# Loading three quarters of a first input tile as rows, turning them on TensorE, and putting all first loads on one queue: a recommender cross network on one Trainium2 core

**Chip, cores, metric.** One core of one Trainium2 chip. The metric is the device time of the whole program in microseconds (us); lower is better. Before the change it was 2277.72 us, the median of three runs (2276.81 to 2277.87).

## The reference

Six layers of a deep-and-cross network on 16384 rows of 1024 features, all in bf16:

```python
B, Din, L = 16384, 1024, 6            # x0 [B, Din], ws [L, Din, Din], bs [L, Din]
x = x0
for l in range(L):
    proj = einsum('bd,de->be', x, ws[l]) + bs[l]
    x = x0 * proj + x
```

## The kernel before

A *unit* is one layer on 1024 rows (a pair of blocks of 512): 16 pairs by 6 layers, 96 units. The 1024x1024 product of a unit is done as seven half-size products P1 to P7 (a Strassen-like scheme), in which VectorE (DVE) forms sums T1 to T4 of input blocks and w5, w6, w7, w3 of weight blocks. This kernel keeps features on partitions, so the first input tile is loaded transposed, in four quarters.

```python
def ttop(name, o, a, b, o_, rd, wr, **kw):          # DVE sums; every tensor_tensor has one line in the profile
    add(name, lambda: tt(o, a, b, o_), rd, wr, **kw)

def group(name, w, bank, bname, rhs, rname, m, start, u=u):   # one product group: 4 matmuls of 128x512
    def fn():
        for k in range(KH):
            nc.tensor.matmul(bank[:], lhsT=wt[(u, w)][:, k, m * P:(m + 1) * P], rhs=rhs[:, k, :],
                             start=(start and k == 0), stop=(k == KH - 1), skip_group_check=True)
    add(name, fn, ...)
# ... cut ...
ttop("T1", T[1][:], B12, B11, SUB, [XI[0, 1], XI[0, 0]], ["T1"])
ttop("T2", T[2][:], B22, T[1][:], SUB, [XI[1, 1], "T1"], ["T2"])
ttop("T3", T[3][:], B22, B12, SUB, [XI[1, 1], XI[0, 1]], ["T3"])
# ... cut: P1, P2 and P5 need B11, B21 and T1; P6 needs T2; P7 needs T3 ...
for i in range(NDUMMY):                              # NDUMMY = 14: matmuls on zeros, one every 0.43 us until about 5.0 us, then every 0.22
    nc.tensor.matmul((pX + pA)[i % (2 * KH)][:], lhsT=zeros[:, 0:P], rhs=zeros[:], start=True, stop=True, ...)

def load_quarter(dh, n):
    nc.sync.dma_start_transpose(out=blk(x0Ts[0], dh, n), in_=x0[n * NB:(n + 1) * NB, dh * H:(dh + 1) * H])

nc.scalar.dma_start(b_rows[:], bs.rearrange("l (m p) -> (l m) p", p=P))
for w in ("1", "2"):
    nc.scalar.dma_start(wt[(0, w)][:], w_src(0, w))
load_quarter(0, 0)
load_quarter(1, 0)
load_quarter(0, 1)
for h in range(2):
    load_half("w12", h)
    load_half("4", h)
load_quarter(1, 1)
```

The order of instructions on each engine comes from a table of ranks, `name@time`. `P6.3` is the fourth group of P6; `2i5`, `2i7`, `2i6` are three small weight sums that later units need. The last unit turns half of its result back on TensorE and stores it in six transfers, of which three are issued last by the SP queue.

## Time and profile before

| | before |
|---|---|
| median time, us | 2277.72 |
| span of the profiled run | 2275.2 |
| PE (TensorE) busy | 2265.4 |
| first P6 matmul | 20.36 |
| issue of the last SP stores to the last byte | 5.36 |

The timeline of DVE (start, duration, engine, line, operation, shapes, and in brackets the idle time and what ended it):

```profile
12.66 1.23 DVE L198 TENSOR_TENSOR T<-x0T 128x2048 bf16<-128x2048 bf16 x1 [3.75 <-DMA x0T<-in_x_dram]
17.23 0.69 DVE L198 TENSOR_TENSOR wp<-w,wp 128x1024 bf16<-128x1024 bf16 x1 [1.70 <-DMA wp<-in_ws_dram]
19.09 1.22 DVE L198 TENSOR_TENSOR T<-x0T,T 128x2048 bf16<-128x2048 bf16 x1
```

These are T1, the second half of w5 and T2, which releases P6.

### The profile page before, as it was taken

Reading aid. Unit: us, or ns where it says so; the run is one execution under the profiler, and the core shown is the slowest. Engines: PE = TensorE matmul, PEld = TensorE weight load, DVE = VectorE, ACT = ScalarE, POOL = GpSimd, SP = SyncE. Lnnn points to the kernel's source line nnn. Section 1 sums busy time; section 2 is a strip of 40 time slices with the busy share of each in tenths; the row PEclk is TensorE's granted clock in tenths of the full one; section 3 lists DMA queues with packets and bytes.
Section 4 is the critical chain, followed back from the end, with each engine's and each line's share of the span. In section 5 each row is a group of like instructions: output and inputs, shape, how many; then the busy total and the mean of one; then the engine's idle time right before and its main releaser. Section 6 shows DMA issues by size and latency. Waiting matters only on the chain.

```text
span 2275.2 us, 34978 instructions
## 1 busy us (share of the span) xinstructions
PE 2265.4 (100%) x12951; PEld 1264.0 (56%) x12951; DVE 2079.9 (91%) x2326; ACT 1839.4 (81%) x3228; POOL 22.1 (1%) x43
## 2 busy tenths in 40 slices
PE   9999999999999999999999999999999999999998
PEld 4455555555555555555555555555555555555554
DVE  7999999999999999999999999999999999999997
ACT  5678888888888888888888888888888888888887
POOL 1110000000000000000000000000000000000000
PEclk9999999999999999999999999999999999999999
DMA  9779797796977969779697796978969689696872
GB/s 279 229 270 289 261 242 269 219 301 209 252 257 221 288 217 260 250 226 283 213 274 241 228 283 204 273 245 230 283 200 292 226 232 286 194 303 216 241 240 65
DMA packets 625868, 557.01 MB, mean 245 GB/s; under 512 B 397600, under 2 KB 552224, under 8 KB 625696
## 3 DMA queue, kind: packets, MB, share of 16 engines
q1 hardware_dynamic: 618864, 534.58, 79.1%
q0 software_dynamic: 5184, 18.88, 2.2%
q8 instruction: 101, 1.65, 0.3%
q10 hardware_dynamic: 1648, 1.32, 0.2%
q14 instruction: 71, 0.58, 0.1%
HBM read 436.22 MB, written 52.43 MB: 215 GB/s over the span
## 4 chain that ended last, share of the span: by engine, by line
PE 98%; DVE 1%; SPq 0%; DMA 0%; issue 0%; ACT 0%; DVEq 0%
PE pA L285 57%; PE pX L389 24%; PE pX L285 16%; DVE ev L198 1%; SPq L529 0%; DMA wp<-in_ws_dram 0%; DVE xst L198 0%; DVE T L198 0%; DVE ti L198 0%; DVE wp L198 0%; SPq L538 0%; ACT ev L294 0%; DVE x0T L487 0%; DVEq L608 0%; DVEq L198 0%
## 5 line engine op out<-in xcount | busy, mean ns | idle before, releaser
L285 PEld LDWEIGHTS <-wp 128*128 128x128 bf16 x7904 | 772.3, 98 | 843.7 <-issue 3.9
L285 PE MATMUL pA<-T,wp 128*128 128x512 bf16 x4608 | 1054.9, 379 | 0.5 <-DVE T L198 0.5
L294 ACT ACTIVATE ev<-pA,b_all 128x512 bf16<-128x512 f32 x1124 | 704.8, 690 | 211.8 <-PE pA L285 211.4
L389 PEld LDWEIGHTS <-wp 128*128 128x128 bf16 x4984 | 487.1, 98 | 156.6 <-issue 15.2
L198 DVE TENSOR_TENSOR ev<-ev,x0T 128x2048 bf16<-128x2048 bf16 (+2 forms) x484 | 482.7, 999 | 8.1 <-ACT ev L294 1.5
L198 DVE TENSOR_TENSOR xst<-ev,xst 128x2048 bf16<-128x2048 bf16 x319 | 388.9, 1219 | 18.6 <-DVE ev L198 0.5
L389 PE MATMUL pX<-ti,wp 128*128 128x256 bf16 x2848 | 397.6, 272 | 0.0
L198 DVE TENSOR_TENSOR ev<-ev,ev 128x2048 bf16<-128x2048 bf16 (+1 forms) x283 | 343.7, 1215 | 26.7 <-ACT ev L294 9.8
L294 ACT ACTIVATE ev<-pX,b_all 128x512 bf16<-128x512 f32 x412 | 289.4, 705 | 59.9 <-PE pX L285 49.3
L285 PE MATMUL pX<-xst,wp 128*128 128x512 bf16 x1376 | 336.4, 379 | 0.0
L285 PE MATMUL pA<-xst,wp 128*128 128x512 bf16 x1280 | 313.5, 379 | 0.0
L290 ACT COPY pX<-pA 128x512 f32<-128x512 f32 x412 | 256.3, 625 | 44.7 <-PE pA L285 44.3
L290 ACT CAST ev<-pX 128x512 bf16<-128x512 f32 x384 | 224.8, 619 | 49.0 <-ACT ev L294 37.6
L198 DVE TENSOR_TENSOR ev<-iu,ip 128x1024 bf16<-128x1024 bf16 x178 | 122.4, 688 | 120.7 <-ACT iu L290 120.7
L290 ACT COPY pX<-pX 128x512 f32<-128x512 f32 x356 | 208.7, 587 | 8.4
L290 ACT CAST iu<-pX 128x512 bf16<-128x512 f32 x356 | 196.8, 639 | 0.0
L198 DVE TENSOR_TENSOR T<-xst 128x2048 bf16<-128x2048 bf16 x160 | 194.8, 1217 | 0.3
L198 DVE TENSOR_TENSOR T<-xst,T 128x2048 bf16<-128x2048 bf16 x160 | 194.5, 1216 | 0.0
L389 PE MATMUL pX<-T,wp 128*128 128x256 bf16 x1068 | 160.2, 273 | 0.0
L290 ACT CAST ip<-pX 128x512 bf16<-128x512 f32 x178 | 104.7, 589 | 54.1 <-PE pX L389 54.1
L389 PE MATMUL pX<-xst,wp 128*128 128x256 bf16 x888 | 133.2, 273 | 0.0
L198 DVE TENSOR_TENSOR xst<-ev,x0T 128x2048 bf16<-128x2048 bf16 x64 | 78.2, 1222 | 1.6
(44 smaller groups left out, 624.3 us busy)
## 6 DMA issues: line engine op xcount, KB each, us to landing
wp<-Lc SPq DMA_DIRECT2D x538, 512.0 KB, 4.6
wp<-in_ws_dram SPq DMA_DIRECT2D x285, 512.0 KB, 5.3
out_dram<-x0T SPq DMA_DIRECT2D x30, 1024.0 KB, 8.6
Lc<-wp POOLq DMA_DIRECT2D x24, 512.0 KB, 6.2
Lc<-isum POOLq DMA_DIRECT2D x12, 512.0 KB, 6.9
w<-in_ws_dram SPq DMA_DIRECT2D x5, 512.0 KB, 6.3
wp<-in_ws_dram ACTq DMA_DIRECT2D x2, 512.0 KB, 5.8
out_dram<-x0T SPq DMA_DIRECT2D x2, 512.0 KB, 3.6
```

The costliest lines, as they stand in the source:

```text
L198: nc.vector.tensor_tensor(out=o, in0=a, in1=b, op=op)
L285: nc.tensor.matmul(bank[:], lhsT=wt[(u, w)][:, k, m * P:(m + 1) * P], rhs=rhs[:, k, :], start=(start and k == 0), stop=(k == KH - 1), skip ...
L290: add(name, lambda: nc.scalar.copy(out=dst, in_=src), rd, wr)
L294: add(name, lambda: nc.scalar.activation(out=dst, in_=src, func=IDENT, bias=b_all[:, c:c + 1], scale=1.0), rd, wr)
L389: nc.tensor.matmul(pX[bank][:, m * NQ:(m + 1) * NQ], lhsT=wv[:, k, m * P:(m + 1) * P], rhs=rhs[:, k, :], start=(start and m == 0 and k == ...
```

## The change

Intent: transposing loads are slow in this trace (245 against 357 GB/s, below), and they hold back the weights behind them. Three quarters of the tile are loaded as plain rows, and TensorE, which has holes at the start (3.2 us among the first 48 matmuls of products, below), turns them by multiplying with the identity. The weights w1 and w2 go between the row loads on the same queue, so that things arrive in the order in which they are used. Six of the 14 dummies go. In the table `t0.1` is a turn on TensorE and `u0.1` the copy of its result; `F` and `E` are ACT's operations on results of products.

```diff
-P1.1@-2.83 P1.0@-1.96 P1.2@-1.10 P1.3@-.24 P2.0@1.27 P2.1@3.53 ...
+t0.0@-4.00 u0.0@-3.70 t0.1@-3.80 u0.1@-3.50 ... t2.0@.3 t2.1@.4 t2.2@2.1 t2.3@2.2 u2.0@.5 ...
+P1.1@-2.83 bT@-2.4 P1.0@-1.96 P1.2@-1.10 P1.3@-.24 P2.1@1.27 P2.0@3.3 ...
-2i5@-9.73 T1@3.57 2i7@4.71 2i6@5.04 c5@5.67 c5b@7.37 c6@8.11 T2@9.25 c7@10.38 T3@11.52 ...
+T1@3.57 c5@5.67 c5b@5.8 c6@5.9 T2@9.25 2i5@9.3 2i7@9.4 2i6@9.5 c7@10.38 T3@11.52 ...
 ... cut: in the same table F1 and E2 are reordered ...
-    NDUMMY = 14
+    NDUMMY = 8
+    TURNED, rows = ((0, 0), (1, 0), (0, 1)), (P1s, U, V)
 ... cut ...
+            for i, (d, n) in enumerate(TURNED):
+                for k in range(KH):
+                    def turn(i=i, k=k, xb=xb):
+                        for j in range(KH):
+                            nc.tensor.matmul(pX[xb][:, j * P:(j + 1) * P], lhsT=rows[i][:, j, k * P:(k + 1) * P], rhs=ident[:], ...)
+                    add(f"t{i}.{k}", turn, [], [Xn[xb]])
+                    cp = nc.vector.tensor_copy if k % 2 else nc.scalar.copy
+                    add(f"u{i}.{k}", lambda ...: cp(out=blk(x0T, d, n)[:, k], in_=pX[xb][:]), ...)
 ... cut: the turn of the bias becomes an operation of the table ...
-    for w in ("1", "2"):
-        nc.scalar.dma_start(wt[(0, w)][:], w_src(0, w))
-    load_quarter(0, 0)
-    load_quarter(1, 0)
-    load_quarter(0, 1)
+    load_rows(0)
+    nc.sync.dma_start(wt[(0, "1")][:], w_src(0, "1"))
+    load_rows(1)
+    load_rows(2)
+    nc.sync.dma_start(wt[(0, "2")][:], w_src(0, "2"))
     for h in range(2):
         load_half("w12", h)
         load_half("4", h)
     load_quarter(1, 1)
```

More of the change, by code (lines that the diff above doesn't have):

```diff
@@ L48 @@
 EARLY = [ranks("""
-P1.1@-2.83 P1.0@-1.96 P1.2@-1.10 P1.3@-.24 P2.0@1.27 P2.1@3.53 P2.2@4.49 P2.3@5.35 P5.1@6.94 P5.0@7.81 P5.3@8.67
+t0.0@-4.00 u0.0@-3.70 t0.1@-3.80 u0.1@-3.50 t0.2@-3.60 u0.2@-3.30 t0.3@-3.40 u0.3@-3.10
+t1.0@-1.90 u1.0@-1.60 t1.1@-1.70 u1.1@-1.40 t1.2@-1.50 u1.2@-1.20 t1.3@-1.30 u1.3@-1.00
+t2.0@.3 t2.1@.4 t2.2@2.1 t2.3@2.2 u2.0@.5 u2.1@.6 u2.2@2.2 u2.3@2.3
+P1.1@-2.83 bT@-2.4 P1.0@-1.96 P1.2@-1.10 P1.3@-.24 P2.1@1.27 P2.0@3.3 P2.2@4.49 P2.3@5.35 P5.1@6.94 P5.0@7.81 P5.3@8.67
 P5.2@9.53 P6.3@10.52 P6.2@11.38 P6.0@12.24 P7.3@13.11 P6.1@13.97 P7.0@14.83 P4.3@15.70 P7.2@16.56 P7.1@17.42
 P4.0@18.29 P4.2@19.15 P4.1@20.01 P3.0@20.88 P3.1@21.74 P3.3@22.60 P3.2@23.47
-F1.0@-.89 E2.0@2.34 F1.1@2.91 F1.3@3.39 F1.2@3.87 E2.1@4.60 E2.2@5.56 E2.3@6.42 E5.3@9.74 E5.0@10.22 F.3@11.59
+F1.1@-.9 F1.0@-.8 F1.2@2.25 F1.3@2.35 E2.1@2.7 E2.0@4.60 E2.2@5.56 E2.3@6.42 E5.3@9.74 E5.0@10.22 F.3@11.59
 E5.2@12.07 E5.1@12.54 F.0@13.31 E7.3@14.18 F.2@14.75 F.1@15.23 E7.0@15.90 E4.3@16.77 E7.2@17.63 E7.1@18.49 E4.2@20.22
 E4.0@20.79 E4.1@21.36 E3.0@21.95 E3.1@22.81 E3.3@23.67 E3.2@24.54
-2i5@-9.73 T1@3.57 2i7@4.71 2i6@5.04 c5@5.67 c5b@7.37 c6@8.11 T2@9.25 c7@10.38 T3@11.52 T4@12.65 2i3@13.79 c3@14.12
+T1@3.57 c5@5.67 c5b@5.8 c6@5.9 T2@9.25 2i5@9.3 2i7@9.4 2i6@9.5 c7@10.38 T3@11.52 T4@12.65 2i3@13.79 c3@14.12
 Qm@15.26 5i5@17.53 Va@19.74 Qa@20.88 Vm@22.01 Wma@23.15 Wmb@23.75 Wx@24.49 Ua@25.63 Um@26.90 Ux@28.17 5i7@29.30
@@ L344, with turn_bias @@
         B11, B12, B21, B22 = blk(xs, 0, 0), blk(xs, 0, 1), blk(xs, 1, 0), blk(xs, 1, 1)
+        A = [f"A{m}" for m in range(KH)]
+        Xn = [f"X{m}" for m in range(KH)]
+        if first:
+            for i, (d, n) in enumerate(TURNED):
+                for k in range(KH):
+                    xb = k if i < 2 else 2 + k % 2
+                    def turn(i=i, k=k, xb=xb):
+                        for j in range(KH):
+                            nc.tensor.matmul(pX[xb][:, j * P:(j + 1) * P], lhsT=rows[i][:, j, k * P:(k + 1) * P], rhs=ident[:],
+                                             start=(j == 0), stop=True, skip_group_check=True)
+                    add(f"t{i}.{k}", turn, [], [Xn[xb]])
+                    cp = nc.vector.tensor_copy if k % 2 else nc.scalar.copy
+                    add(f"u{i}.{k}", lambda cp=cp, d=d, n=n, k=k, xb=xb, x0T=x0T: cp(out=blk(x0T, d, n)[:, k], in_=pX[xb][:]), [Xn[xb]], [Xn[xb], X0[d, n]])
+            def turn_bias():
+                nc.tensor.matmul(pA[KH - 1][:, 0:LK], lhsT=b_rows[:], rhs=ident[0:LK, 0:LK], start=True, stop=True, skip_group_check=True)
+                nc.vector.tensor_copy(out=b_all[:], in_=pA[KH - 1][:, 0:LK])
+            add("bT", turn_bias, [], [A[KH - 1]])
         ttop("T1", T[1][:], B12, B11, SUB, [XI[0, 1], XI[0, 0]], ["T1"])
@@ L348 @@
         ttop("T4", T[4][:], B21, T[2][:], SUB, [XI[1, 0], "T2"], ["T4"])
-        A = [f"A{m}" for m in range(KH)]
-        Xn = [f"X{m}" for m in range(KH)]
         if not one:
@@ L541, with load_rows @@
     nc.scalar.dma_start(b_rows[:], bs.rearrange("l (m p) -> (l m) p", p=P))
-    for w in ("1", "2"):
-        nc.scalar.dma_start(wt[(0, w)][:], w_src(0, w))
-    load_quarter(0, 0)
-    load_quarter(1, 0)
-    load_quarter(0, 1)
+    def load_rows(i):
+        d, n = TURNED[i]
+        nc.sync.dma_start(rows[i][:], x0[n * NB:(n + 1) * NB, d * H:(d + 1) * H].rearrange("(j p) d -> p j d", p=P))
+    load_rows(0)
[3 more added lines that the diff above has]
+    nc.sync.dma_start(wt[(0, "2")][:], w_src(0, "2"))
     for h in range(2):
@@ L550 @@
     load_quarter(1, 1)
-    nc.tensor.matmul(pA[KH - 1][:, 0:LK], lhsT=b_rows[:], rhs=ident[0:LK, 0:LK], start=True, stop=True, skip_group_check=True)
-    nc.vector.tensor_copy(out=b_all[:], in_=pA[KH - 1][:, 0:LK])
     writer, readers, succ, need = {}, {}, [[] for _ in ops], [0] * len(ops)
```

## The prediction

> **What bounds the kernel now.** I read the page first: TensorE (PE) is busy for the whole span, and the chain that ended last is almost all PE.
>
> ```profile
> span 2275.2 us, 34978 instructions
> ...
> PE 2265.4 (100%) x12951; PEld 1264.0 (56%) x12951; DVE 2079.9 (91%) x2326; ACT 1839.4 (81%) x3228; POOL 22.1 (1%) x43
> ...
> PE 98%; DVE 1%; SPq 0%; DMA 0%; issue 0%; ACT 0%; DVEq 0%
> ```
>
> The reader is to see that nothing outside the few microseconds where PE is not on the chain can be won: 2275.2 - 2265.4 = 9.8 us. Next, the view of who waited for whom, restricted to PE over the whole run, says where those are.
>
> ```profile
> PE pX L285 <- ACT pX L290: 1.3, 1, 1.3
> PE pX L526 <- DVE zeros L523: 1.2, 1, 1.2
> PE pA L285 <- DVE T L198: 0.5, 1, 0.5
> PE pX L285 <- DVE wp L198: 0.5, 1, 0.5
> PE pA L285 <- DMA x0T<-in_x_dram: 0.4, 1, 0.4
> ```
>
> Those are all of PE's waits, 3.9 us, and the timeline of PE puts every one before 20.4 us:
>
> ```profile
> 6.78 3.61 PE L285 MATMUL pA<-x0T,wp 128*128 128x512 bf16 x16 [0.36 <-DMA x0T<-in_x_dram]
> 10.52 1.02 PE L285 MATMUL pX<-x0T,wp 128*128 128x512 bf16 x4
> 12.81 2.85 PE L285 MATMUL pX<-x0T,wp 128*128 128x512 bf16 x12 [1.26 <-ACT pX L290]
> 15.59 1.90 PE L285 MATMUL pX<-T,wp 128*128 128x512 bf16 x8
> 17.98 1.90 PE L285 MATMUL pX<-T,wp 128*128 128x512 bf16 x8 [0.49 <-DVE wp L198]
> ```
>
> The columns are start, duration, and in brackets the idle time and what ended it. These are the products P1 (16 matmuls), P2 (16) and P5 (16) of the first unit; P6, the first that needs T2, starts at 20.36 us. Full-speed matmuls start every 0.216 us (the 48 of P6, P7 and P4 start at 20.36 and the next group at 30.72: 10.36 / 48), so these 48 need 10.4 us, yet take 13.58 us from 6.78. The 3.2 us between are what the change can aim at, and what runs before 6.78 (dummies on zeros, 1.19 to 6.2). The chain of waits for the first 31 us names the cause: the SP queue's transposing loads, then a weight load, then VectorE (DVE).
>
> ```profile
> 8.04 2.24 SPq L529
> ...
> 12.05 5.08 DMA wp<-in_ws_dram
> ...
> 17.23 0.70 DVE wp L198
> 17.95 1.23 DVE wp L198
> 19.18 1.15 DVE T L198
> ...
> 20.36 10.52 PE pA L285 x48
> ```
>
> DVE waited 3.7 us for the third transposed quarter (T1 starts at 12.66), then for the halves of w12 and 4, issued only behind the transposes at 10.33 to 12.05 (the first half of the sum w5 starts at 14.84, the second at 17.23); T2 ran at 19.09 and released P6.
>
> [...] In the windows view, 8 to 12 us holds almost only transposing loads and 22 to 30 only plain ones; the last columns are DMA share and GB/s:
>
> ```profile
> 8.00:12.00 4.00, 3.41 (x16) 1.30 (x14) 0.43 (x1) 0.99 (x2) 0.00 (x0) 1.00 1.16 245
> 22.00:30.00 8.00, 8.00 (x39) 3.60 (x37) 8.00 (x10) 6.02 (x11) 0.00 (x0) 1.00 1.09 357
> ```
>
> 245 against 357 GB/s: 512 KB takes 2.1 us transposing and 1.5 us as rows. [...] Here the dummies go every 0.43 us from 1.19 until about 5.0, then every 0.22: 3.8 us. [...] The last unit's transposes by identity agree: four start at 2267.46, the next four at 2267.68, 0.22 / 4 = 55 ns.
>
> **The change part by part.**
>
> *Loads.* Three transposing loads (3 x 2.1 us of DMA) become three row loads (3 x 1.5), and the SP order becomes rows 0, w1, rows 1, rows 2, w2, four half weights, last the one transposed quarter. SP issues take about 0.55 us each (0.51 to 0.58 in the timeline) against 1.5 us to move 512 KB, so DMA is the limit. A copy issued at 10.33 moved its first packets about 1.4 us later; so rows 0, issued at 0.74, should land near 4.1 and the others every 1.55 us: w1 5.6, rows 1 7.2, rows 2 8.7, w2 10.3, halves at 11.1, 11.9, 12.7, 13.5 (before: the last two needed by w5 let it start at 17.23). The transposed quarter adds 2.1 us and a gap of about 1 us: 16.5 (before: just ahead of T2 at 19.09).
>
> *Added on PE.* 3 x 16 = 48 transposes x 55 ns = 2.6 us, against six dummies fewer (14 to 8). The bias turn (0.2) only moves.
>
> *Added on ACT and DVE.* Twelve evictions of 128x512, six each. In the last unit such a cast takes 2.04 / 4 = 0.51 us on ACT and 1.88 / 3 = 0.63 on DVE: 3.1 and 3.8 us, in a stretch (0 to 20.36) where they were busy 7.13 and 6.59 us. ACT now interleaves them with the F1 copies.
>
> *The path in PE's order.* (1) Eight dummies, 1.19 + 8 x 0.427 = 4.6. (2) t0: 4 at half rate (0.43), 12 at 55 ns: 5.7. Its evictions alternate ACT and DVE and end near 6.7, so P1.1 finishes at 7.0 (start of the last matmul 6.8); before, its end was 6.78 + 0.86 = 7.64: only 0.6 us won so far. (3) Bias, P1.0: 8.0. (4) t1, 16 x 55 ns: 8.9. (5) P1.2, P1.3: 10.6. (6) Half of t2: 11.0, P2.1: 11.9 (w2 at 10.3 is in time). (7) Other half of t2, P2.0: 13.2. (8) P2.2 waits for F1.2, which stands on ACT behind the last evictions (12.3 + 0.5 + 0.6): 13.5, ends 14.4. (9) P2.3 15.2, then P5, four groups of 0.864: 18.7.
>
> *DVE beside it.* T1 needs all of t2, whose last eviction ends near 13.2. Full tensor_tensor operations start every 1.14 us: T1 13.2, two halves of w5 at 14.35 and 15.0, w6 15.75, T2 16.9 to 18.1. P5.1 (15.2) and P5.3 (16.9) find their weights ready, and P6 at 18.7 finds T2. T3, behind three small sums (3 x 0.335) and w7, ends near 21.4; P7.3, three groups after P6, wants it at 21.3: a wait of 0.1 us.
>
> *Sum.* P6 moves from 20.36 to about 18.7, less 0.1 us: 1.5 us won. After this PE never waited, so the shift should reach the end if DVE keeps up. DVE gains 1.4 us itself (T1 is later than 12.66 but the waits behind it vanish). The next unit's T1 ended at 40.31 and P5 began at 41.08, a slack of 0.77, more than the 0.1 to 0.3 by which PE may outrun DVE. Nothing in steady state or the tail changes. 2277.7 - 1.5 = 2276.2 us.
>
> **Rivals.**
>
> *A: the transposes take back what the loads give.* 2.6 us of added PE work is close to the 3.2 us of holes. For: they now stand between products, in PE's own order, and rows 0 need a load, a turn and an eviction before the first product. Against: the windows view has PE busy 3.61 of 5 us from 10 and 4.39 of 5.36 from 15, so 2.4 us are free there, and the six dropped dummies give room early. If evictions cost 0.3 us more per stage than I count: 2277.3 to 2277.9.
>
> *B: DVE becomes the bound.* It is busy 24.04 of 24.14 us in the stretch 20.36 to 44.5, so a PE that comes early may meet a DVE that doesn't: T1 starts 0.5 us later than before. For: DVE has no idle time there to catch up. Against: it was idle for 1.70 us before the second half of w5, which goes. PE would wait at P7.3 or the next unit's P5; gain limited to 0.8 us: 2276.9.
>
> *C: everything works as drawn, or better.* If P1.1 starts as soon as its evictions do and nothing waits, PE needs only 4.6 + 2.8 (turns) + 10.4 = 17.8: 2.5 us won, 2275.2. Against: the eviction wait after t0 (about 0.4 us) is in the dependencies.
>
> *D: a cold clock.* With six dummies fewer, the array may not have warmed when P1 starts; a matmul at half rate costs 0.21 us more[...]. For: activity has a hole between t0 and P1.1. Against: dummies and turns run without a break from 1.19 to 5.7, longer than the 3.8 us seen. [...]
>
> **Range and chances.** A and B shorten the gain to 0 to 0.8 us, C lengthens it to 2.5, and three runs before spread over 1.06 us (2276.81 to 2277.87). I take 2274.8 to 2277.7. Two per cent is 45 us, while all of PE's idle time is 9.8 us: faster or slower by over 2% is not credible, 0.5% each for a slow state or an accident.
>
> **What would show each step right or wrong.** Right: P6 (the first pA<-T matmul) starts at 18.2 to 19.2 rather than 20.36; no DVE wait for DMA after T1; PE has no wait after P7.3; the span is shorter by the same amount as P6 moved. Rows load near 350 GB/s. Wrong in the loads: PE waits for rows or w2 by DMA. Wrong in the turns: they start more than 60 ns apart, or PE waits for ACT or DVE evictions for over 1 us in all. Wrong in DVE: a wait for T3 or for T1 of the next unit, with P6 early but the end not. A prediction above 2277.7 would fall if the first P1 matmul came later than 6.8 us or ran at half rate.

2277.7 - 1.5 = 2276.2 us stands on times and rates of the trace before. Of these, the 55 ns of a turn come from the last unit alone, and the gap of about 1 us ahead of the transposed quarter is the stretch from 16 to 17 us, in which the windows view has 56 GB/s. That two weight loads moved to the SP queue change the order of arrival and not the rate was assumed, not shown. The range 2274.8 to 2277.7 was formed from A, B, C and the spread of the runs. That the clock hangs on unbroken work was D's assumption: the trace before shows the dummies every 0.43 us until about 5.0 us and every 0.22 after that.

## More of the kernel before

The timeline of the SP queue has the last stores, and the DMA view of 2262 to 2277 us has the packets moved there:

```profile
2268.22 1.96 SPq L491 DMA_DIRECT2D out_dram<-x0T  x3
```

```profile
DMA packets 5248, 2.62 MB, mean 175 GB/s; under 512 B 2176, under 2 KB 5248, under 8 KB 5248
```

These are all on two queues: 4720 on q1 (what SP issues) and 528 on q10 (what ACT issues).

## The result, and the profile after

The changed kernel took 2277.49 us, the median of four fast runs (2277.26 to 2277.73); the kernel before took 2277.26 in the same rounds (2276.79 to 2277.87). Ratio 1.0001, 95% interval 0.9984 to 1.0018: the same. A ratio here is the mean time of one kernel's fast runs over that of the other's fast runs of the same rounds, so it is not quite the ratio of the medians. The time lies inside the predicted range, but the gain of 1.5 us did not come.

First what holds. The page's head:

```profile
span 2275.9 us, 34833 instructions
...
PE 2254.5 (99%) x12754; PEld 1266.1 (56%) x12993; DVE 2084.2 (92%) x2332; ACT 1844.8 (81%) x3234; POOL 22.1 (1%) x43
```

PE's busy time and count are lower than before only because more matmul records are missing: the weight loads, one for each matmul, are 12993 against 12951, the 42 more that the diff adds (48 turns less 6 dummies). The waits of PE over the run, without the 1.2 us for the zeros at the start:

```profile
PE pX L359 <- DMA ev<-in_x_dram: 0.4, 1, 0.4
PE pA L289 <- DMA wp<-in_ws_dram: 0.4, 1, 0.4
PE pX L289 <- ACT pX L294: 0.2, 1, 0.2
```

With the zeros, four waits of 2.2 us against five of 3.9 us before. The timeline of PE (L359 are the turns, L289 the products):

```profile
5.18 1.07 PE L359 MATMUL pX<-ident,ev 128*128 128x128 bf16 x16 [0.40 <-DMA ev<-in_x_dram]
6.62 1.04 PE L289 MATMUL pA<-x0T,wp 128*128 128x512 bf16 x4 [0.38 <-DMA wp<-in_ws_dram]
...
14.18 1.89 PE L289 MATMUL pX<-x0T,wp 128*128 128x512 bf16 x8 [0.19 <-ACT pX L294]
15.91 3.62 PE L289 MATMUL pX<-T,wp 128*128 128x512 bf16 x15
19.36 4.89 PE L289 MATMUL pA<-T,wp 128*128 128x512 bf16 x21
```

P6, the first product with pA<-T, starts at 19.36 rather than 20.36: 1.0 us won. The chain of waits now begins with a weight load rather than a transposing one:

```profile
1.26 5.32 DMA wp<-in_ws_dram
```

It is w1, landed whole at 6.58. The windows view of the two stretches that the prediction compared:

```profile
8.00:12.00 4.00, 3.95 (x37) 2.56 (x37) 1.46 (x4) 2.41 (x5) 0.00 (x0) 1.00 1.14 322
22.00:30.00 8.00, 7.93 (x37) 3.63 (x38) 8.00 (x11) 5.78 (x11) 0.00 (x0) 1.00 1.09 351
```

(columns: stretch, its length, busy time of PE, PEld, DVE, ACT and POOL with counts, granted clock, DMA share, GB/s). 8 to 12 us moved 322 GB/s rather than 245. Next, a wait that the PE view hides: the timeline of PE's weight loads (PEld) shows the first group of P7 waiting for T3.

```profile
22.13 1.84 PEld L289 LDWEIGHTS <-wp 128*128 128x128 bf16 x10 [0.51 <-DVE T L202]
```

From there the lead is 0.81 us: the group that starts at 169.80 us in the kernel before starts at 168.99.

Now the end. The same views of the tail as before (timeline of SP, then the DMA view of 2262 to 2277 us):

```profile
2268.09 3.10 SPq L513 DMA_DIRECT2D out_dram<-x0T  x3
```

```profile
DMA packets 5249, 2.64 MB, mean 176 GB/s; under 512 B 2176, under 2 KB 5248, under 8 KB 5248
...
q8 instruction: 1, 0.02, 0.4%
```

The last stores are issued 0.13 us earlier than before, yet the packet records put the last byte at 2274.60 against 2273.58: 6.51 us after the issue rather than 5.36. (The issue of the three stores also takes 3.10 us rather than 1.96. In the eight traces with a long tail, listed below, it takes 1.97 to 3.10, in the others 1.93 to 1.96; why is not shown.) One thing is new: a single packet of 16 KB on q8, the queue that fetches instructions. The packet records show it at 2269.29, taking 0.95 us. TensorE has fetched its instructions in such packets all along, one for about 256 of them (25902 matmuls and weight loads, twice the count of loads, to 101 packets before, 25986 to 102 after): 101 before, the last at 2251.0; 102 after, with the last one among the final stores. (That this queue serves TensorE is borne out below: instructions added on TensorE change the count, to 102 in p1 and q1, those added on ACT and DVE do not, 101 in q4.) The windows view shows what is late, first before, then after:

```profile
2273.70:2276.00 2.30, 0.00 (x0) 0.00 (x0) 0.00 (x0) 0.00 (x0) 0.00 (x0) 0.50 0.00 0
```

```profile
2273.70:2276.00 2.30, 0.00 (x0) 0.00 (x0) 0.00 (x0) 0.00 (x0) 0.00 (x0) 0.68 0.03 8
```

After 2273.70 a share of 0.03 of 16 engines for 2.3 us is 1.1 us of one engine. One engine alone finishes about 1 us later than the others, the length of the fetch. (The records do not name the engine of a packet, so that it is the same one is an inference. It is the same in every trace: in the last 0.3 us before the last byte 14 packets end in each of the eight with a fetch there, 108 to 140 in each of the others.)

Between 180 us and the end the lead shrinks further. Comparing each ACT operation's time in the two traces gives eight small steps at fixed places: six of about +0.1 us (at 206, 578, 951, 1156, 1714 and 2066 us), and -0.26 at 1757 and -0.07 at 1985, in sum +0.33. (The rest of the shrinking, 0.36 us, is a slow drift: 23.451 us for a unit against 23.447. The record does not say on which chips these two traces were taken; between c1 and c2 below, on one chip, there is no drift.)

### The profile page after: what moved, and what is told of

Read it like the earlier page. It is cut to its first block, busy times and chain, and to the rows that moved or that the text cites. A ratio compares the mean times of both kernels' runs of the same rounds, so it can differ in the third digit from the quotient of the medians.

```text
span 2275.9 us, 34833 instructions
## 1 busy us (share of the span) xinstructions
PE 2254.5 (99%) x12754; PEld 1266.1 (56%) x12993; DVE 2084.2 (92%) x2332; ACT 1844.8 (81%) x3234; POOL 22.1 (1%) x43
## 3 DMA queue, kind: packets, MB, share of 16 engines
q8 instruction: 102, 1.67, 0.3%
## 4 chain that ended last, share of the span: by engine, by line
PE 98%; issue 1%; DVE 0%; DMA 0%; ACT 0%; DVEq 0%; SPq 0%; ACTq 0%
PE pA L289 57%; PE pX L411 24%; PE pX L289 17%; DVE ev L202 0%; DMA wp<-in_ws_dram 0%; ACT pX L294 0%; PE pX L359 0%; DVE xst L202 0%; DVE x0T L509 0%; ACT ev L298 0%; DVEq L633 0%; ACT x0T L363 0%; SPq L567 0%; PE pA L366 0%; ACTq L294 0%
## 5 line engine op out<-in xcount | busy, mean ns | idle before, releaser
L289 PEld LDWEIGHTS <-wp 128*128 128x128 bf16 x7904 | 772.3, 98 | 840.0 <-issue 1.2
L289 PE MATMUL pA<-T,wp 128*128 128x512 bf16 x4468 | 1047.2, 379 | 7.3
L202 DVE TENSOR_TENSOR xst<-ev,xst 128x2048 bf16<-128x2048 bf16 x319 | 389.1, 1220 | 19.1 <-DVE ev L202 0.9
L289 PE MATMUL pX<-xst,wp 128*128 128x512 bf16 x1371 | 335.9, 379 | 0.3
L289 PE MATMUL pA<-xst,wp 128*128 128x512 bf16 x1205 | 302.4, 379 | 3.9
```

Of the source, the lines that this page charges most:

```text
L202: nc.vector.tensor_tensor(out=o, in0=a, in1=b, op=op)
```

## The experiments

Each run has a short label (c1, p1 and so on), which the text uses from here on.

**Theory F.** The 102nd instruction fetch of TensorE falls among the last stores and costs about 1.0 us, so most of what the start wins is lost. **Rival R.** The longer tail comes from something else in the change (buffers, the order of work at the end). **Theory S**, on the eight steps: they come from the shifted number of ACT and DVE instructions, whose fetches fall elsewhere. P6 below always means the start of its first matmul, and the *tail* the time from the issue of the last SP stores to the last byte. The chips and rounds differ, so each run is compared with the runs of the kernel before that stand beside it.

Two controls ran first, with no edit: the kernel before (c1) and the changed kernel (c2).

> The kernel before, unchanged, as a control. Every theory: ratio 1.000 within 0.0003 of the kernel before; P6 starts near 20.4 us; no instruction fetch for TensorE after 2262 us; the last store's bytes move until about 2273.6 us. What it measures is the run to run noise (0.5 us or so) and how far unit periods (23.447 us here) drift from run to run with no change at all.

> The changed kernel, unchanged, on the same chip. Theory T (the start wins about 0.8 us, and an extra 16 KB instruction fetch for TensorE among the last stores takes about 1 us back[...]): first P6 near 19.4 to 19.5 us, fetch near 2269 us again, tail from the last TensorE matmul to the last byte 1 us longer than in the control, time within 0.3 us of the control. Rival R (the start's lead is lost by chance, slow drift of the unit period and a chance landing at the end): the lead at 180 us is again 0.8 us, no fetch at the end or a fetch without delay, and the time is 0.5 to 0.9 us below the control.

Measured: 2277.03 us for the kernel before (2276.90 to 2277.99), 2277.03 for the changed one (2276.88 to 2277.75), beside 2277.17 (2276.83 to 2277.72, nine runs) of the kernel before; ratio 1.0 for both, 0.9988 to 1.0013. By the traces, on one chip: P6 at 20.32 and 19.60; lead at 150 us 0.52, at the last weight load 0.27 (2269.10 against 2268.83), with the same eight steps between (in sum +0.30); SP issue to last byte 5.34 and 6.37. The tail difference of 1.03 us repeats; the last byte is 0.75 us later. The changed kernel starts better and ends worse. (c2's trace is of the slowest of its five runs, 2277.75 us, so this one is no typical run.)

**More TensorE instructions, nothing else (p1).** The kernel before with its 14 dummies cut into 56 shorter ones of the same total length:

```diff
-    for i in range(NDUMMY):
-        nc.tensor.matmul((pX + pA)[i % (2 * KH)][:], lhsT=zeros[:, 0:P], rhs=zeros[:], ...)
+    for i in range(56):
+        nc.tensor.matmul((pX + pA)[(i // 4) % (2 * KH)][:, 0:128], lhsT=zeros[:, 0:P], rhs=zeros[:, 0:128], ...)
```

> The kernel before with its 14 dummies of 512 columns cut into 56 of 128: the same TensorE time at the start, but 84 more TensorE instructions, exactly as many as the changed kernel has. Theory T: start as in the control (P6 near 20.4 us), but a 16 KB instruction fetch near 2269 us and the last store's bytes 0.7 to 1.0 us later; time 0.5 to 1.0 us above the control. Rival R: no longer than the control (within 0.3 us), since nothing but the dummies differs.

Measured: 2279.39 us (2279.32 to 2279.91) beside 2277.17; ratio 1.001 (0.9997 to 1.0024). The 102nd fetch is there at 2270.9, and the tail is 6.22 us. None of the eight steps appears, though the fetches have moved: for TensorE itself they cost nothing that shows after the start. A second effect is larger: the *first* fetch of TensorE moved from 28.0 to 19.1 us, into the load of the transposed quarter (1,1). T2 then waited 1.45 us for that load, of which 15 of 16 parts had landed by 19.58 and the last at 21.13, and the timeline of PE has

```profile
22.43 2.75 PE L285 MATMUL pA<-T,wp 128*128 128x512 bf16 x11 [2.04 <-DVE T L198]
```

P6 came 2.1 us later than in the control, which the expectation did not foresee. With the tail's 0.9 this is more than the 2.2 us of the medians. To the end of the span rather than to the last byte the tail costs only 0.44 us here (7.47 us from the issue against 7.03 in c1), and that with 2.1 makes the 2.57 us between the two spans. So 84 more instructions (42 matmuls and 42 weight loads), which compute nothing new, slow this kernel by 0.1%: the interval includes 1, but all five runs lie above all nine of the kernel before.

**The changed kernel with the fetch moved away from the tail (p2)**, by more instructions at the start:

```diff
-    for i in range(NDUMMY):
-        nc.tensor.matmul((pX + pA)[i % (2 * KH)][:], lhsT=zeros[:, 0:P], rhs=zeros[:], ...)
+    for i in range(72):
+        nc.tensor.matmul((pX + pA)[(i // 8) % (2 * KH)][:, 0:64], lhsT=zeros[:, 0:P], rhs=zeros[:, 0:64], ...)
```

> The changed kernel with its 8 dummies of 512 columns cut into 72 of 64 (until about 5 us instead of 4.6, where TensorE waited for rows anyway): 128 more TensorE instructions, so that the last instruction fetch comes 64 TensorE pairs earlier, near 2255 to 2263 us, ahead of the last stores. Theory T: first P6 within 0.2 us of the changed kernel, tail as short as in the control, time 0.6 to 1.1 us below the changed kernel and 0.5 to 1.0 below the control. Rival R: the same time as the changed kernel.

Measured: 2276.89 us (2276.74 to 2277.16) beside 2277.17. The last fetch is at 2256.7 and the tail 5.33 us: short again, with all else of the change in place. This speaks for F and against R. But rows 1 came late (PE waited 0.68 us for them until 9.17), P6 stood at 20.06, and the lead was only 0.06 us. The first fetch had come forward to 8.85 us, among the row loads, but it is not shown to be the cause: in b4 below the last of the 16 parts of rows 1 is as late (9.04 us, 0.87 after the one before it; here 9.12 and 0.86), and the first fetch there is at 16.6.

**The kernel before with instructions added only at the end (q1)**, after all work:

```diff
+    for i in range(42):
+        nc.tensor.matmul(pX[0][:, 0:32], lhsT=zeros[:, 0:P], rhs=zeros[:, 0:32], start=True, stop=True, ...)
```

> The kernel before with 42 tiny matmuls (84 TensorE instructions) appended after its last transposes, where TensorE has nothing to do while the last stores run. Theory T (extra fetch): nothing changes up to the last transpose (2269.1 us), but a 16 KB instruction fetch appears among the last stores and the time from the last transpose's weight load to the last store byte grows from 4.44 us to 5.2 to 5.7; time 0.7 to 1.2 us above the kernel before. Rival R (the longer tail of the changed kernel has to do with something else in it, such as the order of its stores' issues): tail 4.4 us and time within 0.3 us of before.

Measured: 2278.69 us (2277.94 to 2278.97) beside 2276.87 (2276.32 to 2277.69, nine runs); ratio 1.0007 (0.9994 to 1.0020). Nothing moved before 2269 us. Timeline of SP, then the new line of the DMA view of 2262 to 2278 us:

```profile
2268.27 1.97 SPq L491 DMA_DIRECT2D out_dram<-x0T  x3
```

```profile
q8 instruction: 1, 0.02, 0.4%
```

The fetch falls at 2270.9, the last byte comes 6.22 us after the issue. Instructions that nothing waits for lengthen the tail by about 0.9 us. The median rose by twice that, 1.8 us, and all five runs lie above all nine beside them; the traced run is the fastest of the five (2277.94), and where the others lost more is not on record.

**The changed kernel with 80 instructions fewer at the very end (q2).** The result is wrong on purpose (relative error 0.166): the turning at the end does one block of four, and the old x is not added.

```diff
-                        for j in range(KH):
+                        for j in range(1):
-                    if nm == "W":
+                    if False:
 ... cut: the turn of V and W then starts its own sum ...
```

> Wrong result on purpose: the changed kernel with 80 TensorE instructions fewer at the end (of the last unit's transposes of V and W only one block in four, and none of the old x), so that its count is 25908 against 25988, near the 25904 of before. Evictions and stores are as they were. Theory T: no fetch after 2262 us, the last store byte 0.8 to 1.2 us earlier than in the changed kernel, time 0.7 to 1.2 us below it and 0.3 to 0.8 below before. Rival R: the tail stays long, time as the changed kernel.

Measured: 2276.00 us (2275.90 to 2276.48) beside 2276.87. No fetch after 2245.8; the last stores are issued at 2267.64 and the last byte is at 2272.97, 5.33 us later. This time the first fetch stayed at 15.9 us, so the good start (P6 at 19.33) and the short tail stand together. The gain of 0.87 us includes some work left out at the end: the lead over the kernel before is 0.56 us at 2262 and the stores are issued about 0.6 us earlier.

**Is the one-queue order needed (q3)?** The changed kernel with w1 and w2 back on the ACT queue:

```diff
-    nc.sync.dma_start(wt[(0, "1")][:], w_src(0, "1"))
+    nc.scalar.dma_start(wt[(0, "1")][:], w_src(0, "1"))
-    nc.sync.dma_start(wt[(0, "2")][:], w_src(0, "2"))
+    nc.scalar.dma_start(wt[(0, "2")][:], w_src(0, "2"))
```

> The changed kernel with w1 and w2 issued by ACT as before, the row loads and turns kept: the turning part alone. Theory Q (the order of arrival on one queue matters[...]): [...] rows 0 lands near 6 us, first turn 0.7 to 1 us later, P6 0.3 to 0.9 us later than in the changed kernel (19.4 to 19.6). Rival: P6 within 0.2 us.

Measured: 2279.71 us (2278.32 to 2280.88) beside 2276.87; ratio 1.0011 (0.9998 to 1.0024).

```profile
7.51 1.89 PE L289 MATMUL pA<-x0T,wp 128*128 128x512 bf16 x4 [1.27 <-DMA wp<-in_ws_dram]
```

Rows 0 were expected to be late and were not (the turns start at 5.17 us, against 5.18 in the changed kernel); w1 was: it landed at 7.47 instead of 6.58, with the loads of the other queue beside it. While PE waited, the array went cold (the granted clock fell from 1.00 to 0.50), which the expectation did not foresee: these four matmuls took 1.89 us where the changed kernel's took 1.04. The windows view has the granted clock in the column after POOL's: 0.99 from 6.0 to 7.5, and then 0.50:

```profile
7.50:10.00 2.50, 2.49 (x7) 0.78 (x8) 0.21 (x1) 0.00 (x0) 0.00 (x0) 0.50 1.09 351
```

By its record the clock was full from 4.05 to 7.46 us and 0.50 from there to 10.88. In the 3.41 us before the fall TensorE was busy for 1.50, with the last dummies and the 16 turns (1.07 us, full rate), and no hole was over 1.27.

P6 came at 21.80, 2.4 us later than in the changed kernel: 0.9 us by the landing of w1 and 1.5 by the half rate of eight matmuls (those of P1.1 and P1.0). So the order is needed, but most of what it saves in this trace is the cold array. No run keeps the transposing loads and changes the order alone, so how the gain at P6 divides between rows and order stays open.

**The eight steps (q4).** The kernel before with four tiny copies on ACT and four on DVE at the start:

```diff
+    scrap = const.tile([P, 8], BF16, name="scrap")
+    for i in range(4):
+        nc.vector.tensor_copy(out=scrap[:, i:i + 1], in_=zeros[:, i:i + 1])
 ...
+    for i in range(4):
+        nc.scalar.copy(out=scrap[:, 4 + i:5 + i], in_=zeros[:, i:i + 1])
```

> The kernel before with four 128x1 copies more on ACT and four on DVE at the start, where both are idle: the same shift of their instruction counts as the changed kernel has, nothing else. Theory S (the eight steps of about 0.1 us at 206, 578, 951, 1156, 1714, 1757, 1985 and 2066 us, by which the changed kernel loses 0.25 us of its lead, come from where ACT's or DVE's instructions fall): the same steps at the same places against the kernel before, net +0.2 to +0.3 us. Rival: no steps, and they come from the SP queue's four more instructions or from the lead itself.

Measured: 2276.94 us (2276.65 to 2277.65) beside 2276.87. Steps at 1757 (-0.27) and 1985 (-0.08) came back; those at 206, 578, 951, 1156, 1714 and 2066 did not, and others came at 1054 (+0.26), 1281 (+0.08) and 1468 (+0.07). The sum is about zero. So two of the eight appear with four more instructions on ACT and on DVE; the origin of the other six stays open. (The version with 56 dummies had none of the eight, those with the changed start, p2 and b4, had all. In q3, which issues two loads on ACT rather than SP, those at 206, 951 and 1714 are 0.28 us instead of 0.1.) Its tail, with 101 fetches of TensorE, is 5.36 us.

**A better version.** Two attempts (b1, b2) to keep the start and lose the late fetch, by 158 empty instructions on TensorE between the products, after the first fetch. The changed kernel ran beside them once more (c3). The second attempt, b2, also moves three small sums behind T4, so that T3 comes earlier:

```diff
+                gcount[0] += 1
+                if gcount[0] > 40 and gcount[0] % 12 == 0:
+                    nc.tensor.nop(nofuse=True)
```

```diff
-T1@3.57 c5@5.67 c5b@5.8 c6@5.9 T2@9.25 2i5@9.3 2i7@9.4 2i6@9.5 c7@10.38 T3@11.52 T4@12.65 2i3@13.79 c3@14.12
+T1@3.57 c5@5.67 c5b@5.8 c6@5.9 T2@9.25 c7@10.38 T3@11.52 T4@12.65 2i5@12.7 2i7@12.75 2i6@12.8 2i3@13.79 c3@14.12
```

> The changed kernel with 158 instructions that do nothing put on TensorE between the products of the whole run (one before every twelfth product after the fortieth), so that the 102nd instruction fetch of TensorE falls some 17 us earlier than 2269, in front of the last stores, while the first fetch stays where it is. The theory that this fetch among the last stores costs about 1.0 us expects from the issue of the last SP store to the last byte 5.3 to 5.4 us rather than 6.4 to 6.5, no fetch after 2262 us, a lead of 0.5 to 0.8 us over the kernel before at 180 us as in the changed kernel, and a median 0.6 to 1.0 us below the changed kernel of the same call. The rival, that the longer tail comes from something else in the change (buffers, order of the stores), expects a tail of 6.2 to 6.5 us again. If the added instructions do not reach the program, the kernel is the changed kernel again and all numbers repeat.

> As the previous one, and the three small weight sums 2i5, 2i7 and 2i6, which stand on VectorE between T2 and T3, moved behind T4. Expected: T3 comes about 1.0 us earlier, the wait of P7.3 for T3 (0.15 us of TensorE, 0.5 us of its weight load) is gone, the lead at 180 us is 0.15 to 0.2 us larger than in the previous one, unless a product of the second unit then waits for one of the moved sums; the median 0.1 to 0.2 us below the previous one. A rival: VectorE is the limit there and the lead is unchanged, because the small sums only wait elsewhere.

> The changed kernel once more, on the chip and in the rounds of the two versions beside it. Expected: a median within 0.5 us of the kernel before, last fetch at about 2269 us, tail 6.3 to 6.5 us, first product P6 at 19.3 to 19.6 us.

Measured, beside 2277.52 us of the kernel before (2277.21 to 2278.64, nine runs): b1 2278.00 (2277.29 to 2279.43), b2 2277.64 (2277.28 to 2277.90), the changed kernel (c3) 2277.79 (2277.39 to 2278.07). As tests of the fetch, b1 and b2 failed: such empty instructions were not in the built program (97 semaphore instructions on TensorE in both, as in the changed kernel), and the last fetch fell at 2270.1 and 2268.6 with tails of 6.42 and 6.40 us. b1 is therefore the changed kernel once more, and it showed something else. Its profiled run (2279.43 us) starts like this:

```profile
5.59 1.89 PE L363 MATMUL pX<-ident,ev 128*128 128x128 bf16 x16 [0.80 <-DMA ev<-in_x_dram]
7.27 1.91 PE L293 MATMUL pA<-x0T,wp 128*128 128x512 bf16 x4
```

Turns and P1.1 ran at half rate (1.07 and 1.04 us in the profile after), and P6 came at 20.89. Of the five runs two are at 2277.3 to 2277.4 and three at 2278.0 to 2279.4; only one of the three was profiled, so only for that one is the cold array shown.

b2 shows the other small step. In its timeline of DVE, T3 starts at 20.30 us, against 21.17 in c3, and P7 waits less for it. b2's P6 was 0.14 us later (19.81 against 19.67) and its last weight load 0.05 us earlier: 0.19 us won by the order of three small sums.

**The same with instructions that stay in the program (b4)**, increments of a semaphore that nobody reads:

```diff
+    gcount = [0]; pad = tc.alloc_semaphore("pad")
 ...
+                gcount[0] += 1
+                if gcount[0] > 40 and gcount[0] % 12 == 0:
+                    nc.tensor.sem_inc(pad)
```

> The do-nothing instructions of b1 and b2 turned out not to be in the built program (97 semaphore instructions on TensorE in both, as in the changed kernel), so b1 only repeated the changed kernel and b2 only moved the small sums. Here the same places get an increment of a semaphore that nobody reads, and the built program has 161 instructions more on TensorE (258 of this kind); the small sums stand behind T4 as in b2. The theory that the 102nd instruction fetch among the last stores costs about 1.0 us expects: the last fetch some 15 to 20 us earlier (2249 to 2255), from the issue of the last SP store to the last byte 5.3 to 5.4 us rather than 6.3 to 6.5, and, with the start of the changed kernel (P6 at 19.3 to 19.8 us, no wait at P7.3), a median 0.7 to 1.4 us below that of the kernel before in the same rounds, if the increments cost TensorE nothing. The rival, that another thing in the change lengthens the tail, expects 6.2 to 6.5 us there. If each increment holds TensorE for 10 ns or more, the lead shrinks by 1.6 us or more along the run and the kernel is slower than before.

Measured: 2276.64 us (2276.43 to 2276.78) beside 2276.93 (2276.72 to 2278.51, nine runs); ratio 0.9998 (0.9984 to 1.0012). The last fetch moved to 2251.4. Timeline of SP, with the last byte at 2273.29:

```profile
2268.00 1.93 SPq L517 DMA_DIRECT2D out_dram<-x0T  x3
```

5.29 us rather than 6.26 in the changed kernel's third trace. The increments cost TensorE nothing that can be seen: apart from the T3 step there is none against that trace. The start of this run was not the best (rows 1 came late, PE waited 0.49 us for them, P6 at 19.86), so the median falls 0.29 us below that of the kernel before, less than the 0.7 to 1.4 hoped for. All five of its runs lie below that median; so did all five of p2 (-0.28). The interval calls both the same as the kernel before, so a better version is likely but not established.

All correct traces together, tail measured from the issue of the last SP stores to the last byte:

| trace | fetches of TensorE | last one at, us | tail, us |
|---|---|---|---|
| before, c1, q4 | 101 | 2251.0, 2250.9, 2251.7 | 5.36, 5.34, 5.36 |
| p2, b4 | 102 | 2256.7, 2251.4 | 5.33, 5.29 |
| after, c2, c3, b1, b2 | 102 | 2269.3, 2268.5, 2268.6, 2270.1, 2268.6 | 6.51, 6.37, 6.26, 6.42, 6.40 |
| p1, q1, q3 | 102 | 2270.9, 2270.9, 2271.4 | 6.22, 6.22, 6.01 |

From the issue to the end of the span rather than to the last byte, the five traces with a short tail need 7.00 to 7.05 us and the eight with a long one 7.26 to 8.09, 7.7 on average. So of a last byte that is about 1 us late, 0.2 to 1.1 us reaches the end, 0.7 on average.

The tail follows the fetch, not the version: the kernel before has it long with more instructions (p1, q1), the changed one has it short with the fetch elsewhere (p2, b4). R has fallen. What decides is how many instructions TensorE runs, and where: with 25902 or 25906 matmuls and weight loads (before, q2) there are 101 fetches, with 25986 (after, p1, q1, q3) there is one more and it falls at the end, and with 26114 (p2) or 25986 and 161 semaphore instructions (b4) it falls 12 to 18 us earlier.

## Why the prediction was right and wrong

The time lies in the stated range and the class came out as said, but by luck: of the 1.5 us that were to be won about 1.0 was won at P6 (0.7 in the controls), and about as much was lost again later, in a way that the text ruled out.

- **Failed: "Nothing in steady state or the tail changes."** The 42 matmuls (with 42 weight loads) added at the start brought a 102nd instruction fetch among the last stores, and the last byte came about 1.0 us later after their issue (1.15 in the first pair of traces, 1.03 in the controls on one chip; to the end of the span 0.74 and 1.02). q1 adds the fetch alone, p2 and b4 move it away. Steady state changed by +0.3 us through the eight steps, of which only two are explained.
- **Mis-sized: the loads.** The interval was right: rows 0, w1, rows 1, rows 2 and w2 have their *first* of 16 parts in SBUF at 4.06, 5.53, 7.04, 8.54 and 10.08, against 4.1, 5.6, 7.2, 8.7 and 10.3 in the text. But the consumers waited for the last part, and that landed at 5.13, 6.58, 8.07, 9.57 and 11.13, about 1.05 us later (the turns began at 5.18, P1.1 at 6.62). PE waited 0.40 us for rows 0 and 0.38 for w1, both absent from the text. The start of P1.2 was to be 8.9 and was 9.48 (its first matmul is missing from the trace, so the timeline puts it at 9.70; its weight load is at 9.43); from P2.1 on the lateness stays at 0.7, and P6 came at 19.36, not 18.7.
- **Right: the turns.** 16 turns took 0.89 us in the chain, 55 ns each. P2.2's wait for the copy on ACT was foreseen (0.3 us) and measured 0.19. P6, in 18.2 to 19.2 by the text's own test, missed narrowly at 19.36.
- **Right in kind, a little larger: T3.** A wait of 0.1 us was foreseen; b2 puts it at 0.19. That is the only part of rival B (DVE as the bound) that was seen. DVE's own chain was 0.7 to 0.8 us late as well (T1 at 13.97 rather than 13.2, T2 at 17.58 rather than 16.9), and T2 ended at 18.80: a P6 at 18.7 would have met it 0.1 us early.
- **Rival A** (turns eat the gain): not seen. Four waits of 2.2 us remain, and those that are new are loads, not evictions. **Rival C**: not seen in any run. **Rival D** (a cold clock) was rejected for the changed kernel because "dummies and turns run without a break". There is a break, 0.2 to 0.8 us, where rows 0 are late (without one only in c2 and p2). In b1 and q3 P1.1 then ran at half rate, and P6 came 1.2 us later than in c3 (same program as b1) and 2.4 later than in the profile after. It is not the usual case: of the other six traces with this start, four (after, c3, b2, b4) turned and multiplied at full rate, and two were partly cold (turns of 1.89 us in c2 and 1.38 in q2, P1.1 of 1.36 and 1.26). The break alone does not decide it: c2 has none and is partly cold, c3 and b2 have one of 0.67 and 0.81 us and are not. The record of the granted clock has the first full rate at 4.05 us in q3, at 4.41 to 5.64 in after, c3, b2, b4 and q2, at 6.93 in c2 and at 9.17 in b1. (The windows view prints 1.00 before the first such record.)

For c2 against c1, in one line: 0.72 us won at P6, 0.52 left at 150 us (T3, and small shifts), 0.27 left at the last weight load (steps), less 1.03 in the tail: the last byte 0.75 us later. The medians of these two agree within 0.01 us all the same: c2's traced run is 0.7 us above its median, c1's is the median. Runs of one kernel in one call lie 0.35 to 1.8 us apart, in b1 and q3 over 2. And a trace ends 1.23 to 1.26 us after its last byte where that byte belongs to an SP store (after, c3, b2, p1, q3) and 1.67 to 1.72 where it belongs to the ACT store (all other correct traces); only q2 (ACT store, 1.26) falls out of this, and why it is so is not shown. Hence the causes above rest on the traces. The medians alone (+0.23, -0.14 and +0.27 us for the changed kernel) do not tell a gain from a loss.

Open: the six steps; why rows land up to half a microsecond apart between profiled runs of one start; the two values of the last stretch; how much of the gain at P6 comes from the rows and how much from the order of loads.

## What to carry to other kernels

When a kernel is tuned to fractions of a microsecond, count the instructions of each engine as well as their time: this long unrolled program fetched its own code by DMA (102 packets of 16 KB for TensorE), and one more fetch among the last stores cost about as much there (1.0 us) as the change had won at P6; where a fetch fell into p1's load of the transposed quarter, T2 waited 1.45 us. Look for it in the packets at the end, since the chain of waits did not show it here, and try to move it by instructions in the busy middle, where 161 semaphore increments cost nothing that could be seen (b4: last fetch at 2251.4, tail 5.29 us). In estimates of a load, take the landing of its last part, here about 1.05 us after the first, and do not count on a warm-up to end at a fixed time: with this start the first full rate came anywhere from 4.05 to 9.17 us.
